# A two-branch spectral and gated-MLP kernel: transposes of nine row blocks moved to DMA, the row DFT one pass later, and the first unit's z differences on VectorE

## The chip, the cores and the metric

The kernel runs on one core of one Trainium2 chip. A core has five engines that run their own instruction queues and meet through semaphores: TensorE (PE; its weight loads are listed as PEld), VectorE (DVE), ScalarE (ACT), GpSimd (POOL) and SyncE (SP), which here only issues DMA transfers. ScalarE and GpSimd issue some transfers too. The metric is the device time of one execution in microseconds (us); lower is better. All times below come from runs of the kernel before, or from one profiled execution of it.

## The reference: what is computed

The input x is a matrix of 2048 rows by 576 columns, normalised row by row (xn). Two branches read xn. The first is a global filter: a two-dimensional real FFT, a product with a complex weight, and the inverse FFT. The second is a gated MLP with a product over the rows (w_sp). The result is x plus the first branch times the SiLU of the second:

```python
x = A_x
xn = _layernorm(x, axis=-1)
s = irfft2(rfft2(xn) * (w_r + 1j * w_i))               # branch A
z = gelu(xn @ w_in)                                    # 2048 x 4608
z1 = z[..., :Fh]; z2 = _layernorm(z[..., Fh:])         # Fh = 2304
g = w_sp @ z2 + b_sp[:, None]
g = silu((z1 * g) @ w_out)                             # branch B
return x + s * g
```

## The kernel before, in words

**Rows.** The 2048 rows are 16 blocks of 128 (MT = 16), called rows m here. A block is loaded into XC, normalised by VectorE into one of three buffers XN (m % 3), transposed, and kept as xnT for both branches. The steps of a row are:

- `ln1_stats` and `ln1_aggr` (lines 270 and 274): mean and variance on VectorE. The reciprocal root comes from GpSimd in two small instructions (`rstd_of`, lines 261 and 263), for row 0 from ScalarE and a VectorE reciprocal.
- `ln1_apply` (lines 293 and 296): two VectorE instructions write XN.
- `xpose` (lines 304 and 305): five TensorE transposes into PSUM, and a ScalarE copy into xnT.
- `p0_fold` (lines 311 and 312): sum and difference of the two halves of the row, on VectorE. Four buffers FS.
- `p0` (line 329), `p0_tail` (line 321), `p0_out` (lines 334 and 336): the DFT along the row as four full products and two row-tiled ones (64 rows each[...]), a ScalarE copy out of PSUM, and a store to DRAM that GpSimd issues.

**Column stages.** `p1` to `p5` do the DFT over the rows, the filter, and the inverse transforms, with DRAM in between. They are separated by stretches that only hold other work, so that the transfers can land.

**Chunks of branch B.** The products with w_in are 168 chunks: 96 of z2 (line 458, 384 columns wide, ordered by row) and 72 of z1 (line 554, which need all rows). The string `kinds` gives their order, and `fill(n, lead, tails, ahead)` issues the next n of them at a place in the program. Chunks go in groups of four: of the first two the full products, then one row-tiled pass for the remainders of all four, then the full products of the other two. What is given as `ahead` is issued before the row-tiled pass, and `tails` right behind it. After each chunk `z2_stats(lead)` may put statistics or normalisations of z2 on VectorE, as far as the sums kept by `spend` (the program's own estimate of the load of TensorE and VectorE) allow within `lead`.

**The row loop** (from line 781) does, for row m: fold of m, statistics of m + 3, normalisation of m + 2, and two chunks. An even row's `p0` comes between its two chunks, an odd row's ahead of them. Transposes run one row ahead. Four chunks are issued before the loop and 28 in it.

**The transition** (lines 856 to 873). After the column stages come the products with w_sp. They use sums and differences of quarters of w_sp ("slabs", brought in transposed by DMA; `slab_sums`, line 540, in three parts) and of z2 (`tsum`, lines 601, 603 and 605). `main(u)` (line 617) does unit u: seven groups of eight products into three PSUM tiles. Its fourth group adds to a tile that VectorE must have read first (the addition p1a, line 621), and uses the difference of line 603.

**Order.** The instructions of SyncE, TensorE and VectorE are in the order of the program text (`tc.manual_schedule`); those of ScalarE and GpSimd are ordered by the compiler's scheduler. Every engine runs its instructions in order.[...]

Of the kernel before, what the change touches and what calls it, by code (L numbers as in the profile page):

```python
# [90 lines left out]
def kernel(  # L91
# [138 lines left out]
    def load_win_main(t, fs, eng=nc.sync):  # L230
        for a in range(2):
            eng.dma_start(out=t[:, a:KS - 1:2, :], in_=wv[a, 0:2 * P, fs].rearrange("(b p) f -> p b f", p=P))
# [15 lines left out]
    for m0, m1 in ((0, 1), (1, 2), (2, 4)):  # L248
        nc.sync.dma_start(out=XC[0][:, m0:m1, :], in_=xv[:, m0:m1, :])
    for n in range(2):  # L250
        load_win_main(WIN2[:, :, n * ZC:(n + 1) * ZC], slice(Fh + n * ZC, Fh + (n + 1) * ZC), nc.scalar)
    for g in range(3):
        (load_win if g else load_win_tail)(WIN2[:, :, 2 * g * ZC:2 * (g + 1) * ZC], slice(Fh + 2 * g * ZC, Fh + 2 * (g + 1) * ZC))
        if g == 0:
            nc.sync.dma_start(out=CDSD, in_=cd_cdsd.ap().rearrange("p (a k l) -> p a k l", a=2, k=3))
        load_x(g + 1)
    nc.sync.dma_start(out=G1, in_=cd_g1.ap().rearrange("p (s k) -> p s k", s=N2))

    def rstd_of(mv, n, tag):
        ve = small.tile([P, n], F32, tag=tag + "v")  # L260
        nc.gpsimd.tensor_scalar(out=ve[:], in0=mv[:, :, 1], scalar1=1e-5, scalar2=one[:, 0:1], op0=ALU.add, op1=ALU.mult)
        rs = small.tile([P, n], F32, tag=tag + "r", bufs=5)
        nc.gpsimd.tensor_tensor(out=rs[:], in0=ve[:], in1=mhalf[:, 0:n], op=ALU.pow)
        return rs
# [7 lines left out]
    def ln1_aggr(m):  # L272
        mv = small.tile([P, 1, 2], F32, tag="mv1", bufs=5, name="mv1")
        nc.vector.bn_aggr(out=mv[:, 0, :], in_=st1[m][:])
        if m == 0:
            rs = small.tile([P, 1], F32, tag="l11r", bufs=5, name="rs1")
            nc.scalar.activation(out=rs[:], in_=mv[:, :, 1], func=ACT.Sqrt, bias=eps[:], scale=1.0)
        else:
            rs = rstd_of(mv, 1, "l11")
        ln1_of[m] = (mv[:, 0, 0:1], rs[:, 0:1])  # L280
# [4 lines left out]

    st1 = {}
# [13 lines left out]
    def xpose(m):  # L300
        xn = XN[m % 3]
        pt = psh.tile([P, KS, P], BF16, tag="h")
        for ks in range(KS):
            nc.tensor.transpose(pt[:, ks, :], xn[:, ks * P:(ks + 1) * P], ident[:])
        nc.scalar.activation(out=xnT[:, m, :, :], in_=pt[:], func=ACT.Identity)  # L305
# [287 lines left out]
    def tsum(u, which):  # L593
# [6 lines left out]
        if which == 0:  # L600
            nc.vector.tensor_tensor(out=t, in0=zblk(p, 1, 1), in1=zblk(p, 0, 1), op=ALU.subtract)
        elif which == 1:
            nc.vector.tensor_tensor(out=t, in0=t2, in1=zblk(p, 0, 0), op=ALU.subtract)
        else:
            nc.gpsimd.tensor_tensor(out=t, in0=zblk(p, 1, 0), in1=t2, op=ALU.subtract)  # L605
# [91 lines left out]
    kinds = "2" * 32 + "221" * 11 + "21" * 20 + "221" * 9 + "2111" * 4  # L697
# [42 lines left out]
    with tc.manual_schedule(engines={SP, PE, DVE}):  # L740
# [20 lines left out]
        nc.scalar.activation(out=THF[:, 0:1], in_=ln1_of[0][1], func=ACT.Gelu_apprx_tanh)  # L761
        xpose(0)
        ln1_stats(1, (1,))
        ln1_aggr(1)
        keep_warm(2)
        fill(1, 0)
        ln1(2)
        ln1_apply(1)
        p0_fold(0)
        ln1_apply(2)  # L770
        ln1(3)
        fill(1, 0, lambda: p0_pair(0), lambda: (xpose(1), p0(0, True), xpose(2)))
        p0_fold(1)
        ln1_apply(3)
        p0(1, False)
        p0_out(1)
        ln1(4)
        fill(1, 0)
        fill(1, 0)
        nc.sync.dma_start(out=MM, in_=cd_mm.ap().rearrange("p (a k) -> p a k", a=3))  # L780
        for m in range(2, MT):
            if m % 2 == 0:
                xpose(m + 1)
            spend(0.78, 2.35 if m + 3 < MT else 0.6)
            p0_fold(m)
            if m + 3 < MT:
                ln1(m + 3)
            if m + 2 < MT:
                ln1_apply(m + 2)
            if m % 2 == 0:  # L790
                fill(1, 0)
                p0(m, True)
                fill(1, 0, lambda: p0_pair(m))
            else:
# [3 lines left out]
                if m + 1 < MT:  # L798
                    xpose(m + 1)
                fill(1, 0)  # L800
            if m in (6, 9):
                load_win1(m // 9)
# [18 lines left out]
        for hh in range(0, N2, 2):  # L821
# [4 lines left out]
            if hh % 8 != 6:  # L826
                fill(1)
# [5 lines left out]
        for u in range(4 * NLC):  # L833
            p4(u)
            spend(0.45, 1.22 if u % 2 == 0 else 0)
            if u % 3 != 2:
                fill(1)
# [19 lines left out]
        for i in range(NT // P):  # L857
            fill(1, 2)
            slab_sums(i, 0, 1)
            spend(0, 0.75)  # L860
        later.append(partial(slab_sums, 2, 0, 2))
        fill(max(kinds.rindex("2") + 1 - place[0], 0), 2)
        nc.sync.dma_start(out=BB, in_=B_b_sp.rearrange("(a s) -> a s", a=1).to_broadcast((P, S)))
        fill(len(kinds) - place[0], 3)
        z1_store(None, None)
        tick[0] += 4
        z2_stats(99)
        assert not stats_q and not norm_q
        for w in (0, 2, 1):
            tsum(0, w)  # L870
# [51 lines left out]
```

## Time and profile before

| | us |
|---|---|
| median of 10 runs | 502.81 |
| lowest and highest | 502.15, 504.59 |
| profiled execution | 502.94 |
| its span on the core | 501.2 |
| TensorE busy | 488.6 |
| VectorE busy | 343.1 |
| GpSimd busy | 210.5 |
| ScalarE busy | 169.4 |

The span is the time from the first to the last instruction of the profiled execution; about 1.7 us of the execution lie around it. Busy times of TensorE are modelled: a matmul counts until its modelled end, so short waits don't show. The profile gives for each group of instructions the engine, the source line, what is written and read, and, in brackets, how long the engine stood idle before it and what released it. The granted clock of TensorE is at its full value throughout (0.998 on average). The transfers of the first 30 us keep the DMA engines busy; after that, up to the column stages, they are mostly idle.

### The profile page before, as it was taken

The page shows a single profiled execution, that of the slowest core. Times are in us where ns is not written, and L with a number is a line of the kernel's source. Part 1 is how long each engine was busy: PE and PEld are TensorE (multiplying, and loading weights), DVE is VectorE, ACT ScalarE, POOL GpSimd, SP SyncE. Part 2 cuts the span into 40 slices and gives each one's busy share as a digit, 9 for nine tenths or more (in the row PEclk, how much of TensorE's full clock was granted, in tenths as well). Part 3 has the DMA queues.
Part 4 walks back from the last instruction along what each step waited for, and adds up shares of the span by engine and source line. Part 5 has one row for each costly group of instructions (what it writes and reads, how often), then busy time and mean ns, then how long its engine had stood idle before and what let it go on. Part 6 is the DMA issues. An engine that isn't in the chain of part 4 may idle for free.

```text
span 501.2 us, 9370 instructions
## 1 busy us (share of the span) xinstructions
PE 488.6 (97%) x3454; PEld 308.7 (62%) x3454; DVE 343.1 (68%) x746; ACT 169.4 (34%) x355; POOL 210.5 (42%) x281
## 2 busy tenths in 40 slices
PE   6999999999999999799999999999999999999996
PEld 2555454555556544366666677666666678888885
DVE  5766588898655798966665547865656637877734
ACT  3887778686778556200000011000000011000001
POOL 2664323444242675554534501445354301666600
PEclk9999999999999999999999999999999999999999
DMA  7951688977362999771112499021111863111202
GB/s 233 335 174 61 221 290 238 333 226 231 125 232 91 241 229 269 212 232 60 35 33 64 115 159 233 25 63 33 40 57 33 173 135 94 50 48 45 79 27 70
DMA packets 86766, 70.67 MB, mean 141 GB/s; under 512 B 39776, under 2 KB 79328, under 8 KB 86464
## 3 DMA queue, kind: packets, MB, share of 16 engines
q1 hardware_dynamic: 80480, 55.54, 41.4%
q0 software_dynamic: 5008, 13.71, 8.3%
q10 hardware_dynamic: 1232, 0.82, 0.6%
q8 instruction: 27, 0.44, 0.3%
q14 instruction: 19, 0.16, 0.1%
HBM read 40.40 MB, written 21.26 MB: 123 GB/s over the span
## 4 chain that ended last, share of the span: by engine, by line
PE 88%; ACT 5%; DMA 3%; DVE 2%; issue 1%; SPq 0%; ACTq 0%; DVEq 0%
PE pm L617 42%; PE ph L554 13%; PE po L671 13%; PE ph L458 12%; ACT AR L334 2%; PE pb L386 2%; PE pa L329 2%; DMA AR<-in_A_x_dram 1%; ACT Z L477 1%; PE pa L428 1%; DMA Z1d<-AR 1%; PE pa L374 1%; ACT AR L305 1%; ACT Z L471 1%; DMA AR<-c_cdsd 1%
## 5 line engine op out<-in xcount | busy, mean ns | idle before, releaser
L617 PE MATMUL pm<-AR,Z 128*128 128x384 bf16 (+1 forms) x864 | 138.9, 309 | 0.0
L621 DVE TENSOR_TENSOR AR<-pm,AR 128x384 f32<-128x384 f32 (+3 forms) x162 | 82.4, 513 | 70.0 <-PE pm L617 66.8
L617 PE MATMUL pm<-AR 128*128 128x384 bf16 (+1 forms) x648 | 107.1, 309 | 2.9 <-DVE AR L621 2.3
L617 PEld LDWEIGHTS <-Z 128*128 128x128 bf16 x864 | 84.5, 98 | 40.6
L458 PE MATMUL ph<-AR 128*128 128x384 bf16 (+1 forms) x480 | 90.1, 327 | 1.8 <-ACT AR L305 0.9
L554 PE MATMUL ph<-AR 128*128 128x512 bf16 (+1 forms) x360 | 85.9, 380 | 0.0
L617 PEld LDWEIGHTS <-AR 128*128 128x128 bf16 x648 | 63.3, 98 | 33.9 <-issue 2.8
L631 ACT ACTIVATE AR<-pm 128x384 f32<-128x384 f32 (+1 forms) x27 | 12.3, 455 | 188.5 <-PE pm L617 188.5
L671 PE MATMUL po<-AR 128*128 128x288 bf16 x540 | 66.6, 287 | 0.0
L671 PEld LDWEIGHTS <-AR 128*128 128x128 bf16 x594 | 56.9, 98 | 14.0
L605 POOL TENSOR_TENSOR AR<-Z,AR 128x1024 bf16<-128x1024 bf16 x27 | 57.9, 2143 | 14.3 <-PE pm L617 13.4
L458 PEld LDWEIGHTS <-AR 128*128 128x128 bf16 (+1 forms) x480 | 40.0, 97 | 37.1 <-issue 15.6
L574 POOL DMA_DIRECT2D Z1d<-AR x55 | 32.0, 582 | 58.5 <-ACT AR L563 54.2
L632 POOL TENSOR_TENSOR AR<-AR 128x384 f32<-128x384 f32 (+1 forms) x27 | 22.9, 849 | 75.6 <-ACT AR L631 75.3
L554 PEld LDWEIGHTS <-AR 128*128 128x128 bf16 (+1 forms) x360 | 30.2, 97 | 28.1 <-issue 5.5
L563 ACT ACTIVATE AR<-ph 128x512 bf16<-128x512 f32 x72 | 42.1, 593 | 15.6 <-PE ph L554 15.4
L477 ACT ACTIVATE Z<-ph 128x384 bf16<-128x384 f32 x66 | 32.0, 502 | 24.6 <-PE ph L458 24.3
L674 ACT ACTIVATE TH<-po 128x576 f32<-128x576 f32 x15 | 9.8, 650 | 77.8 <-PE po L671 77.8
L635 POOL TENSOR_TENSOR AR<-AR 128x384 f32<-128x384 f32 (+1 forms) x27 | 30.4, 1126 | 12.7 <-DVE AR L621 12.6
L485 DVE BATCH_NORM_STATS2 st<-Z 128x6 f32<-128x384 bf16 x66 | 32.5, 545 | 1.5 <-ACT Z L477 1.5
L628 DVE TENSOR_TENSOR AR<-AR 128x384 bf16<-128x384 bf16 (+1 forms) x108 | 31.8, 336 | 0.9
L680 DVE SCALAR_TENSOR_TENSOR AR<-TH,po 128x576 bf16<-128x576 f32 x15 | 11.3, 755 | 30.0 <-ACT TH L674 29.9
(82 smaller groups left out, 476.8 us busy)
## 6 DMA issues: line engine op xcount, KB each, us to landing
Z1d<-AR POOLq DMA_DIRECT2D x55, 128.0 KB, 3.8
AR<-Z1d SPq DMA_DIRECT2D x36, 192.0 KB, 3.0
AR<-in_A_x_dram SPq DMA_DIRECT2D x18, 144.0 KB, 2.8
AR<-in_B_w_out_dram SPq DMA_DIRECT2D x1, 2592.0 KB, 9.9
Ad<-AR POOLq DMA_DIRECT2D x16, 144.5 KB, 3.0
AR<-Ad SPq DMA_DIRECT2D x4, 578.0 KB, 5.8
AR<-in_A_w_r_dram SPq DMA_DIRECT2D x16, 144.5 KB, 3.6
AR<-in_A_w_i_dram SPq DMA_DIRECT2D x16, 144.5 KB, 3.7
```

The costliest lines, as they stand in the source:

```text
L458: nc.tensor.matmul(self.ph[:], lhsT=xnT[rows, self.m, ks, :], rhs=WIN2[rows, ks, n * ZC:(n + 1) * ZC], start=start, stop=stop)
L477: nc.scalar.activation(out=zc, in_=ph[:], func=ACT.Gelu_apprx_tanh)
L485: nc.vector.bn_stats(out=z2s[m][:, n, :], in_=zc)
L554: nc.tensor.matmul(self.ph[:].rearrange("p (a t) -> p a t", a=4), lhsT=wb[rows, ks, (fi % WG) * P:(fi % WG + 1) * P], rhs=xnT[rows, 4 * tq ...
L563: nc.scalar.activation(out=zs, in_=ph[:], func=ACT.Gelu_apprx_tanh)
L574: (nc.sync if place[0] > len(kinds) - 16 else nc.gpsimd).dma_start(out=d, in_=s_)
L605: nc.gpsimd.tensor_tensor(out=t, in0=zblk(p, 1, 0), in1=t2, op=ALU.subtract)
L617: nc.tensor.matmul(dst, lhsT=z[:, s, :], rhs=SLB[SA[name]][:, s, 0:nt], start=(s == 0 and not more), stop=(s == HM - 1), skip_group_check= ...
L621: nc.vector.tensor_tensor(out=out, in0=x, in1=y, op=ALU.add)
L628: nc.vector.tensor_tensor(out=o, in0=o, in1=zb[:, f, h, 0:nt], op=ALU.mult)
L635: nc.gpsimd.tensor_tensor(out=ux, in0=p1a, in1=B[0], op=ALU.add)
L671: nc.tensor.matmul(pv[:, hh, :], lhsT=U[:, fi, h, i * P:(i + 1) * P], rhs=WOUT[:, fi, c0 + hh * H2:c0 + hh * H2 + w // nh], start=(fi == 0 ...
```

## The change

Four things are changed.

1. **Start.** The loads are re-ordered. The first weights of z2 come in halves between the first rows; ScalarE issues one of them where it issued four, and SyncE the other three. Row 3 comes behind the tails of the weights. The z1 weights of the first two groups follow the last rows directly; before, the constants G1 followed, then MM, and the z1 weights came at rows 6 and 9. G1 is now loaded in halves at rows 9 and 11, and MM after the loop. Rows 0 and 1 both take their root from ScalarE, and rows 2 and 3 take the addition of epsilon on VectorE. The first transpose is copied by VectorE.
2. **Row loop.** It begins with row 0, behind four chunks, and holds 32 chunks. Row m now folds m, normalises m + 4 and takes the statistics of m + 5. Transposes run three rows ahead. From row 7 (`DT`) on they are DMA transposes from XN to xnT, issued by SyncE, with no TensorE or ScalarE work. An even row's `p0` is given as `ahead`, so it comes behind both chunks' full products. `kinds` begins with 36 z2 chunks.
3. **Column stages.** Two chunks of the filter stage are issued later, and the chunks among the inverse products over the rows (`p4`) have a lead of 0.6.
4. **Transition.** The last z2 statistics and the first difference of unit 0 come before the last four chunks, the other two differences right behind these, and all three run on VectorE for unit 0.

```diff
@@ -227,8 +227,8 @@
     HT = H2 - 2 * P
     wv = B_w_in.rearrange("(a d) f -> a d f", a=2)
 
-    def load_win_main(t, fs, eng=nc.sync):
-        for a in range(2):
+    def load_win_main(t, fs, eng=nc.sync, halves=(0, 1)):
+        for a in halves:
             eng.dma_start(out=t[:, a:KS - 1:2, :], in_=wv[a, 0:2 * P, fs].rearrange("(b p) f -> p b f", p=P))
 
     def load_win_tail(t, fs):
@@ -245,20 +245,30 @@
         load_win(wb, fs)
 
     nc.scalar.dma_start(out=ident[:], in_=cd_id.ap())
-    for m0, m1 in ((0, 1), (1, 2), (2, 4)):
-        nc.sync.dma_start(out=XC[0][:, m0:m1, :], in_=xv[:, m0:m1, :])
-    for n in range(2):
-        load_win_main(WIN2[:, :, n * ZC:(n + 1) * ZC], slice(Fh + n * ZC, Fh + (n + 1) * ZC), nc.scalar)
+    wh = [(WIN2[:, :, n * ZC:(n + 1) * ZC], slice(Fh + n * ZC, Fh + (n + 1) * ZC)) for n in range(2)]
+
+    def load_row(m):
+        nc.sync.dma_start(out=XC[0][:, m, :], in_=xv[:, m, :])
+
+    load_row(0)
+    load_win_main(*wh[0], nc.scalar, (0,))
+    nc.scalar.activation(out=THF[:, 1:2], in_=eps[:], func=ACT.Sqrt)
+    load_win_main(*wh[0], nc.sync, (1,))
+    load_row(1)
+    load_win_main(*wh[1], nc.sync)
+    load_row(2)
     for g in range(3):
         (load_win if g else load_win_tail)(WIN2[:, :, 2 * g * ZC:2 * (g + 1) * ZC], slice(Fh + 2 * g * ZC, Fh + 2 * (g + 1) * ZC))
         if g == 0:
+            load_row(3)
             nc.sync.dma_start(out=CDSD, in_=cd_cdsd.ap().rearrange("p (a k l) -> p a k l", a=2, k=3))
         load_x(g + 1)
-    nc.sync.dma_start(out=G1, in_=cd_g1.ap().rearrange("p (s k) -> p s k", s=N2))
-
-    def rstd_of(mv, n, tag):
+    for g in range(2):
+        load_win1(g)
+
+    def rstd_of(mv, n, tag, eng=nc.gpsimd):
         ve = small.tile([P, n], F32, tag=tag + "v")
-        nc.gpsimd.tensor_scalar(out=ve[:], in0=mv[:, :, 1], scalar1=1e-5, scalar2=one[:, 0:1], op0=ALU.add, op1=ALU.mult)
+        eng.tensor_scalar(out=ve[:], in0=mv[:, :, 1], scalar1=1e-5, scalar2=one[:, 0:1], op0=ALU.add, op1=ALU.mult)
         rs = small.tile([P, n], F32, tag=tag + "r", bufs=5)
         nc.gpsimd.tensor_tensor(out=rs[:], in0=ve[:], in1=mhalf[:, 0:n], op=ALU.pow)
         return rs
@@ -272,17 +282,18 @@
     def ln1_aggr(m):
         mv = small.tile([P, 1, 2], F32, tag="mv1", bufs=5, name="mv1")
         nc.vector.bn_aggr(out=mv[:, 0, :], in_=st1[m][:])
-        if m == 0:
+        if m < 2:
             rs = small.tile([P, 1], F32, tag="l11r", bufs=5, name="rs1")
             nc.scalar.activation(out=rs[:], in_=mv[:, :, 1], func=ACT.Sqrt, bias=eps[:], scale=1.0)
         else:
-            rs = rstd_of(mv, 1, "l11")
+            rs = rstd_of(mv, 1, "l11", nc.vector if m < 4 else nc.gpsimd)
         ln1_of[m] = (mv[:, 0, 0:1], rs[:, 0:1])
 
     def ln1(m):
         ln1_stats(m)
         ln1_aggr(m)
 
+    DT = 7
     st1 = {}
     ln1_of = {}
 
@@ -297,12 +308,18 @@
                                 in0=xr[:, None, :, 2 * P:H2].to_broadcast((P, 2, 2, HT)), scalar1=mean, scalar2=rs,
                                 op0=ALU.subtract, op1=ALU.mult)
 
-    def xpose(m):
+    def xpose_dma(m):
+        nc.sync.dma_start_transpose(out=xnT[:, m, :, :], in_=XN[m % 3].rearrange("p (k i) -> p k i", k=KS))
+
+    def xpose(m, eng=nc.scalar):
         xn = XN[m % 3]
         pt = psh.tile([P, KS, P], BF16, tag="h")
         for ks in range(KS):
             nc.tensor.transpose(pt[:, ks, :], xn[:, ks * P:(ks + 1) * P], ident[:])
-        nc.scalar.activation(out=xnT[:, m, :, :], in_=pt[:], func=ACT.Identity)
+        if eng is nc.scalar:
+            nc.scalar.activation(out=xnT[:, m, :, :], in_=pt[:], func=ACT.Identity)
+        else:
+            eng.tensor_copy(out=xnT[:, m, :, :], in_=pt[:])
 
     Adw = Ad[:].rearrange("(c m p) l -> m p c l", c=2, p=P)
 
@@ -602,7 +619,7 @@
         elif which == 1:
             nc.vector.tensor_tensor(out=t, in0=t2, in1=zblk(p, 0, 0), op=ALU.subtract)
         else:
-            nc.gpsimd.tensor_tensor(out=t, in0=zblk(p, 1, 0), in1=t2, op=ALU.subtract)
+            (nc.gpsimd if u else nc.vector).tensor_tensor(out=t, in0=zblk(p, 1, 0), in1=t2, op=ALU.subtract)
 
     def main(u):
         it, p = units[u]
@@ -694,7 +711,7 @@
     zq = iter(range(MT * NZC))
     yq = iter(range(FT * 4))
     tick = [0]
-    kinds = "2" * 32 + "221" * 11 + "21" * 20 + "221" * 9 + "2111" * 4
+    kinds = "2" * 36 + "221" * 10 + "21" * 20 + "221" * 8 + "2111" * 4
     kinds += "2" * (MT * NZC - kinds.count("2")) + "1" * (FT * 4 - kinds.count("1"))
     held = []
     place = [0]
@@ -758,48 +775,49 @@
         ln1_stats(1, (0,))
         nc.vector.reciprocal(out=ln1_of[0][1], in_=ln1_of[0][1])
         ln1_apply(0)
-        nc.scalar.activation(out=THF[:, 0:1], in_=ln1_of[0][1], func=ACT.Gelu_apprx_tanh)
-        xpose(0)
         ln1_stats(1, (1,))
         ln1_aggr(1)
+        nc.scalar.activation(out=THF[:, 0:1], in_=ln1_of[1][1], func=ACT.Gelu_apprx_tanh)
+        xpose(0, nc.vector)
+        nc.vector.reciprocal(out=ln1_of[1][1], in_=ln1_of[1][1])
+        ln1_apply(1)
         keep_warm(2)
         fill(1, 0)
+        xpose(1)
         ln1(2)
-        ln1_apply(1)
-        p0_fold(0)
+        fill(1, 0)
+        ln1(3)
         ln1_apply(2)
-        ln1(3)
-        fill(1, 0, lambda: p0_pair(0), lambda: (xpose(1), p0(0, True), xpose(2)))
-        p0_fold(1)
-        ln1_apply(3)
-        p0(1, False)
-        p0_out(1)
         ln1(4)
         fill(1, 0)
+        ln1_apply(3)
+        xpose(2)
         fill(1, 0)
-        nc.sync.dma_start(out=MM, in_=cd_mm.ap().rearrange("p (a k) -> p a k", a=3))
-        for m in range(2, MT):
-            if m % 2 == 0:
-                xpose(m + 1)
-            spend(0.78, 2.35 if m + 3 < MT else 0.6)
+        for m in range(MT):
+            if m % 2 == 0 and m + 3 < DT:
+                xpose(m + 3)
+            spend(0.9 if m + 3 < DT else 0.6, 0.5 + 0.6 * (m + 4 < MT) + 1.0 * (m + 5 < MT))
             p0_fold(m)
-            if m + 3 < MT:
-                ln1(m + 3)
-            if m + 2 < MT:
-                ln1_apply(m + 2)
+            if m + 4 < MT:
+                ln1_apply(m + 4)
+                if m + 4 >= DT:
+                    xpose_dma(m + 4)
+            if m + 5 < MT:
+                ln1(m + 5)
             if m % 2 == 0:
                 fill(1, 0)
-                p0(m, True)
-                fill(1, 0, lambda: p0_pair(m))
+                fill(1, 0, lambda: p0_pair(m), lambda: p0(m, True))
             else:
                 p0(m, False)
                 p0_out(m)
                 fill(1, 0)
-                if m + 1 < MT:
-                    xpose(m + 1)
+                if m + 3 < DT:
+                    xpose(m + 3)
                 fill(1, 0)
-            if m in (6, 9):
-                load_win1(m // 9)
+            if m in (9, 11):
+                hf = slice((m - 9) * N2 // 4, (m - 7) * N2 // 4)
+                nc.sync.dma_start(out=G1[:, hf, :], in_=cd_g1.ap().rearrange("p (s k) -> p s k", s=N2)[:, hf, :])
+        nc.sync.dma_start(out=MM, in_=cd_mm.ap().rearrange("p (a k) -> p a k", a=3))
         for ch in range(4):
             p1_read(ch)
         load_w(0)
@@ -823,7 +841,7 @@
             if hh + 2 < N2:
                 p2(hh + 2)
                 spend(0.25, 1.5)
-            if hh % 8 != 6:
+            if hh % 8 != 6 and hh < 26:
                 fill(1)
             p3(hh)
             spend(0.5)
@@ -834,7 +852,7 @@
             p4(u)
             spend(0.45, 1.22 if u % 2 == 0 else 0)
             if u % 3 != 2:
-                fill(1)
+                fill(1, 0.6)
         js = [4 * g + r + 2 * h for g in range(MT // 4) for r in range(2) for h in range(2)]
         slabs = [(a, i) for i in range(NT // P) for a in (0, 2, 1, 3)]
         for n in range(0, MT, 2):
@@ -854,20 +872,20 @@
                 slab_sums((n - 6) // 4, 0, 0)
                 spend(0, 1.5)
         load_z1(0)
-        for i in range(NT // P):
-            fill(1, 2)
-            slab_sums(i, 0, 1)
-            spend(0, 0.75)
-        later.append(partial(slab_sums, 2, 0, 2))
-        fill(max(kinds.rindex("2") + 1 - place[0], 0), 2)
-        nc.sync.dma_start(out=BB, in_=B_b_sp.rearrange("(a s) -> a s", a=1).to_broadcast((P, S)))
-        fill(len(kinds) - place[0], 3)
-        z1_store(None, None)
         tick[0] += 4
         z2_stats(99)
+        tsum(0, 0)
+        later.append(partial(slab_sums, 2, 0, 2))
+        assert place[0] > kinds.rindex("2")
+        nc.sync.dma_start(out=BB, in_=B_b_sp.rearrange("(a s) -> a s", a=1).to_broadcast((P, S)))
+        for i in range(NT // P):
+            fill(1)
+            slab_sums(i, 0, 1)
+        fill(len(kinds) - place[0])
+        z1_store(None, None)
+        for w in (1, 2):
+            tsum(0, w)
         assert not stats_q and not norm_q
-        for w in (0, 2, 1):
-            tsum(0, w)
         for i in range(2):
             slab_sums(i, 0, 2)
         nc.sync.dma_start(out=WOUT, in_=B_w_out.rearrange("(f p) d -> p f d", p=P))
```

## The prediction

> **What bounds the kernel now.** I read the busy row of TensorE over the span first, then busy times by stage, then the chain of waits inside each stage where TensorE is not full.
>
> ```profile
> PE   6999999999999999799999999999999999999996
> 0.00:15.00 15.00, 10.62 (x59) 4.88 (x60) 8.61 (x32) 7.30 (x12) 3.48 (x14) 1.00 0.81 247
> 15.00:51.00 36.00, 35.42 (x292) 20.97 (x291) 25.50 (x91) 28.54 (x56) 22.31 (x39) 1.00 0.58 176
> 200.00:215.00 15.00, 12.21 (x70) 6.17 (x68) 14.35 (x21) 3.42 (x7) 8.84 (x8) 1.00 0.77 235
> ```
>
> The windows' columns are PE, PEld, DVE, ACT and POOL busy, granted clock, DMA share, GB/s. The kernel is TensorE work from end to end except in two places: the first 15 us (4.4 us idle) and 200 to 215 us (2.8 us idle). The change touches both, and the stage between 15 and 51 us, the row DFT, which looks full. There the chain shows a short wait that the busy time hides, because matmul ends are modelled:
>
> ```profile
> 20.26 0.61 ACT AR L305
> 20.86 0.02 issue
> 20.89 0.30 DVE AR L311
> 21.19 0.05 issue
> 21.24 0.67 PE pa L329 x4
> ```
>
> This is one row's path: ScalarE copies the transposed row (L305), VectorE folds it (L311), TensorE multiplies (L329). The fours of L329 for even rows stand at 21.24, 26.44, 31.65, 36.85, 42.05 and 47.26: 5.20 us for a pair of rows. TensorE's last instruction before 21.24 starts its four matmuls at 20.33, and four of these take 0.65 from start to start elsewhere (18.47 to 19.12), so it waits 0.26 us. Of the other 4.94, two groups of five transposes take 0.28 each (24.32 to 24.60). Without them a pair costs 4.38.
>
> Next, VectorE at the start of the stage, where it once has the order that the changed loop will have throughout:
>
> ```profile
> 11.95 0.21 DVE L274 BATCH_NORM_AGGREGATE mv<-st 128x2 f32<-128x12 f32 x1
> 12.08 0.24 DVE L311 TENSOR_TENSOR AR<-AR 128x256 bf16<-128x256 bf16 x1
> 13.32 0.41 DVE L293 TENSOR_SCALAR AR<-AR,mv,rs 128x512 bf16<-128x512 bf16 x1 [0.80 <-POOL rs L263]
> 13.87 0.81 DVE L270 BATCH_NORM_STATS2 st<-AR 128x6 f32<-128x288 bf16 x2
> 14.72 0.21 DVE L274 BATCH_NORM_AGGREGATE mv<-st 128x2 f32<-128x12 f32 x1
> 15.03 0.38 POOL L261 TENSOR_SCALAR ve<-mv,one 128x1 f32<-128x1 f32 x1 [1.75 <-DVE mv L274]
> 15.50 0.55 POOL L263 TENSOR_TENSOR rs<-ve,mhalf 128x1 f32<-128x1 f32 x1
> ```
>
> Statistics, fold, then the normalisation of that same row, which waits for GpSimd's reciprocal root: 1.37 us from the aggregate at 11.95 to the normalisation at 13.32. GpSimd's result for the next row, at 16.05, is 1.33 us behind its aggregate. In the rest of the stage another row's work lies between the two and nothing waits.
>
> Last, the 2.8 us at 206 to 211:
>
> ```profile
> 206.25 2.57 POOL L605 TENSOR_TENSOR AR<-Z,AR 128x1024 bf16<-128x1024 bf16 x1 [2.53 <-PE pm L617]
> 206.75 2.61 DVE L540 TENSOR_TENSOR AR<-AR 128x1024 bf16<-128x1024 bf16 x1
> 210.60 0.54 DVE L621 TENSOR_TENSOR AR<-pm,AR 128x384 f32<-128x384 f32 x1
> 211.20 1.46 PE L617 MATMUL pm<-AR 128*128 128x384 bf16 x8 [2.26 <-DVE AR L621]
> ```
>
> TensorE waits for the addition L621, which stands behind two block sums (L540) on VectorE. One of these takes 2.61 us beside a GpSimd difference; alone they take 0.63.
>
> [...]
>
> **The change, part by part.**
>
> 1. Start. The loads are re-ordered: row 0, half of the first weights, row 1, the rest. ScalarE issues one weight load in place of four, so its table load (3.35, 1.28 us) comes about 1.7 us earlier; row 0's root still waits for its aggregate, which ends at 4.21, and gains 0.4 us at most. But row 1's statistics stand on VectorE ahead of row 0's reciprocal, and row 1 now has 392 KB of weights ahead of it. At about 250 GB/s (the first 15 us show 247) it lands near 5.3 instead of 3.7. So row 0 is normalised near 6.0 (5.17 before), and the first product is near 7.9 (7.10). VectorE copies transpose 0 from PSUM; nearest row, ScalarE's 0.68. Later this start loses less: the weight waits at 8.14 and 9.13 and the constants' wait at 11.09 (0.9 and 0.6 us) go, since both come earlier. What decides is rows 4 to 7 (590 KB): the bytes ahead of them are the same as before, where they landed at 12.7; their issue comes about a microsecond sooner, so I take 12.1. Row 4's statistics then start at 12.1, its normalisation at 14.4, row 5's statistics at 15.0. Before, row 5's started at 15.20. For VectorE the start is a wash, with 1 us either way.
>
> 2. Row loop. Each iteration is now: fold of row m, normalisation of m+4, statistics of m+5. On VectorE's queue the statistics of a row are followed by one fold and then by the normalisation of that row. That is the order seen at 11.95. One row costs 0.85 (statistics to aggregate) + 1.37 + 0.55 (normalisation to the next statistics, 13.32 to 13.87) = 2.77 us, 5.54 per pair, against 5.20 now. From row 5 to row 15: 15.0 + 10 x 2.77 = 42.7. GpSimd is in order too, and issuing one DFT store costs it 0.75 (two in 1.49). The order of instructions puts a store between the two steps of rows 6 and 14 (0.75 each) and stores of rows 4 to 6 ahead of row 11, the last of which needs row 6's product; I take 1.0. That makes 45.2 for row 15's statistics, 42.12 before.
>
> Behind it: the fold of row 11 ends 1.4 later, 46.6; then its products and two chunks (0.5 + 1.3) and two pairs at 4.38, which makes 57.2. Before, at that amount of work: products of row 15 at 49.19, with the two chunks 51.0, and the four chunks that the new stage holds more (4 x 0.65 + 0.43) make 54.0. So the stage loses 3.2 us, although 45 transposes (9 x 0.28 = 2.5 us of TensorE) and nine ScalarE copies are gone: they are taken out of a stage that then waits for VectorE. Moving an even row's products behind the second chunk removes the 0.26 us wait, already counted in 4.38.
>
> 3. The nine DMA transposes. SyncE reaches the first behind the twelve loads of the first z1 weights, which now follow x directly. SyncE stalls with eight outstanding (the last z1 weights went out at 27.51, when the 1 MB load issued at 17.72 landed), so I take 26.8 for its turn. Each then costs SyncE between 0.8 us (1.30 for the w_sp ones, scaled from 1,024 to 640 columns)[...]. I take 0.9 and 3 us to land (w_sp: 3.2 to 8.0, median 4.4). Row 7 lands near 30 and its buffer is wanted near 31.9: hidden. The rest follow at VectorE's pace. Of the moved loads, G1 and MM are wanted at 61 us or later: hidden.
>
> 4. Transition. From 202.29 VectorE does two block sums, a difference, three sums, two differences, two sums: 7 x 0.63 + 3 x 0.71 = 6.5, 208.8, then the addition, 209.35. GpSimd's bias addition (1.08 us at 209.05 before) will now run beside some of these: up to 0.7 more (the second L540 ran to 1.39 beside it). I take 209.7 for the waiting products, a gain of 1.5. Next late is still the same addition: two sums stay ahead of it.
>
> 5. Fill chunks taken from the column stages are spent later, same number; the smaller lead of the fills among the inverse column products may save some of the 0.5 us that TensorE waits at 150 to 160. I take 0.4 for this.
>
> Sum: +3.2 - 1.5 - 0.4 = +1.3 us on the profiled execution's 502.94 (span 501.2 plus 1.7 around it), which is 0.13 above the median of the runs: **504.1**.
>
> **The rivals.**
>
> - TensorE-bound row loop (faster). If GpSimd's root returned within a fold (0.4 us), VectorE would need 1.8 to 1.9 a row and TensorE decides: from 14.2, 4.66 + 4.94 + 6 x 4.38 gives 50.1, a gain of 3.9, with the rest 5.8: 497.1. For it: 45 transposes less and the chain's own path cut. Against: both 1.37 and 1.33.
> - GpSimd's stores don't hit (no change). Without their 2.5 us the stage loses 0.7, and the total is 501.7, at the edge of no change. For it: row 11's wait rests on one product's time.
> - Slow transposes (much slower). The last must land before row 15's products at 55.6, so 26.8 + 9s + 3 decides from s = 2.9 us per issue; at 3.5 the stage ends 6.2 later still: 510.3. For it: [...]single issues of 2.65 in the trace. Against: a median of 1.30.
>
> **How the numbers follow.** Chances: forecast 0.50, stores hidden 0.20, TensorE-bound 0.18, slow transposes 0.12. The forecast's own range is 502.8 to 506.3 (start 1 us either way, GpSimd 1 us, transition 0.5). The range 499.5 to 508.5 leaves out about half of the first and last rivals. Slower by over 0.2% (1 us, about what can be told from no change): nine tenths of the forecast and slow transposes, 0.56; within: 0.20; faster: TensorE-bound and a third of the stores' case, 0.24.
>
> **What would show it.** In the new profile: normalisations in the row loop idle "<-POOL rs", rows 2.8 us apart, TensorE's products of odd rows waiting for the fold; no wait on the transposes; the products after the first unit's third waiting about 0.8 us instead of 2.26. If rows follow at 2.2 us, steps 2 and its stores are wrong. If the first chain item behind a fold is a DMA, step 3 is.

## The result and the profile after

The changed kernel takes 512.83 us (median of 9 runs, 511.90 to 513.71); the kernel before, in the runs beside it, 502.48. The ratio is 1.0196, with a 95% interval of 1.0179 to 1.0212: some 10 us slower, where 504.1 was forecast and 508.5 was the upper end of the range. The profiled execution has a span of 510.6 us, 9.4 more than before. Each experiment below ran beside the kernel before, whose median lay between 501.35 and 502.48 us, so kernels are compared by their ratios.

TensorE's row of the page shows two new places. The second to fourth of its 40 slices (13 to 51 us, the row loop) have 8, 7 and 7 tenths where the kernel before has 9. In the sixth (64 to 77 us) the engine first stands still and then has a slow clock:

```profile
PE   6877969999999999999999999999999999999997
PEclk9999979999999999999999999999999999999999
```

Five stretches of the changed kernel, with PE, PEld, DVE, ACT and POOL busy, granted clock, DMA share and GB/s:

```profile
64.00:68.00 4.00, 3.61 (x22) 1.60 (x20) 0.00 (x0) 3.97 (x12) 2.11 (x4) 1.00 0.44 142
68.00:72.00 4.00, 0.22 (x2) 0.13 (x2) 0.00 (x0) 0.46 (x2) 0.54 (x1) 0.76 0.78 245
72.00:76.00 4.00, 4.00 (x14) 1.84 (x13) 1.30 (x3) 1.25 (x2) 0.54 (x1) 0.50 1.01 413
76.00:80.00 4.00, 4.00 (x24) 2.02 (x23) 2.43 (x5) 2.73 (x5) 0.82 (x2) 0.89 0.61 157
208.00:222.00 14.00, 13.37 (x80) 6.45 (x79) 12.38 (x24) 5.66 (x11) 6.46 (x10) 1.00 0.74 226
```

From 68 to 72 us TensorE does next to nothing (it waits 4.17 us, up to 71.78); from 72 to 76 it counts as full, but with 14 matmuls where 24 follow in the next 4 us, at a clock of 0.50. The last line is the transition, which has become better: 0.6 us idle, where the kernel before had 2.8.

The two waits by name (in total, times, longest) are TensorE's for the folds of the row loop and its wait ahead of `p1`:

```profile
PE pa L346 <- DVE AR L328: 7.0, 6, 1.9
PE pa L367 <- DMA AR<-Ad: 4.2, 1, 4.2
```

The chain of waits of the changed kernel tells where the 4 us come from (start, length, what):

```profile
53.90 8.30 DVE st L502 x18
...
62.22 0.33 DVE mv L518
...
62.65 0.26 POOL ve L271
...
62.99 0.48 POOL rs L273
...
63.52 0.45 POOL Ad L353
...
64.27 0.56 POOL Ad L353
...
64.99 2.82 DMA Z1d<-AR
67.81 3.93 DMA AR<-Ad
...
71.78 0.64 PE pa L367 x2
72.42 1.71 PE ph L571 x4
```

Read it backwards. The first product of `p1` (L367) waits for a reading of Ad (67.81); the readings wait for the last stores of Ad (L353, the chain names the landing by the store of Z1d that is next in the queue); and these two stores, of rows 14 and 15, are issued at 63.52 and 64.27, although row 15's products end near 57. They stand in GpSimd's queue behind the reciprocal root (L271, L273) of the second norm's row 0. That root needs VectorE's aggregate (L518), which needs 18 statistics that VectorE could only begin behind its last fold. In the kernel before, the same two stores were issued at 50.77, ahead of that root at 57.12:

```profile
50.77 1.55 POOL L336 DMA_DIRECT2D Ad<-AR  x2 [3.73 <-ACT AR L334]
...
57.12 0.26 POOL L261 TENSOR_SCALAR ve<-mv,one 128x1 f32<-128x1 f32 x1 [1.71 <-DVE mv L501]
```

No line of the change touches either; GpSimd's order is the compiler's.

In the row loop the forecast's picture is there. VectorE's timeline, with the idle time before an instruction in brackets:

```profile
36.41 0.41 DVE L304 TENSOR_SCALAR AR<-AR,mv,rs 128x512 bf16<-128x512 bf16 x1 [1.98 <-POOL rs L273]
...
39.19 0.41 DVE L304 TENSOR_SCALAR AR<-AR,mv,rs 128x512 bf16<-128x512 bf16 x1 [0.81 <-POOL rs L273]
...
45.52 0.41 DVE L304 TENSOR_SCALAR AR<-AR,mv,rs 128x512 bf16<-128x512 bf16 x1 [1.60 <-POOL rs L273]
...
53.41 0.29 DVE L328 TENSOR_TENSOR AR<-AR 128x256 bf16<-128x256 bf16 x1 [2.83 <-DMA AR<-AR]
```

A row's normalisation waits 0.8 us for GpSimd, more where a store stands between, and the last fold waits 2.83 us for a DMA transpose.

To compare whole kernels I counted TensorE's lost time: the time from the first matmul to a stage's first product, less what the matmuls in between need at 2.4 columns a nanosecond, half of it for row-tiled ones. Both are estimates from the trace of the changed kernel: four matmuls of 512 columns take 0.86 us from start to start (209.61 to 210.47 us), which is 2.38 columns a nanosecond, and four row-tiled ones of 384 columns take 0.34 us (55.40 to 55.74), where sixteen full ones take 2.60 (52.21 to 54.81). The twelve warm-up products at the start count as lost. Lost time in us, stage by stage, in one profiled execution each:

| kernel | row stage | to p1 | p1 to p2 | p2 to p4 | p4 to p5 | p5 to w_sp | behind |
|---|---|---|---|---|---|---|---|
| before | 12.8 | 0.8 | 2.4 | 4.0 | 2.1 | 2.4 | 8.7 |
| after | 19.2 | 5.2 | 4.6 | 4.2 | 2.9 | 2.4 | 6.8 |
| stores on SyncE | 19.3 | 0.8 | 2.1 | 4.2 | 2.9 | 2.3 | 6.5 |
| statistics first | 12.2 | 7.4 | 5.0 | 4.3 | 2.9 | 2.3 | 6.8 |
| both mends | 11.7 | 0.8 | 2.1 | 4.2 | 2.8 | 2.4 | 9.6 |
| no DMA transposes | 16.3 | 0.8 | 2.1 | 4.3 | 2.9 | 2.3 | 6.5 |
| before, normalisation first | 16.4 | 0.8 | 2.4 | 4.0 | 2.1 | 2.4 | 8.1 |
| transition alone | 11.9 | 0.8 | 2.4 | 4.0 | 2.1 | 2.4 | 6.5 |

The 45 transposes that went to DMA save 2.4 us of work (45 x 53 ns, 128 columns at that pitch; in the trace of the kernel before five take 0.28 us, 24.32 to 24.60, or 56 ns each). So after against before: +6.4 - 2.4 = +4.0 in the row stage, +4.3 in the wait ahead of p1, +2.2 in the slow clock, +0.2 from p2 to p4, +0.8 in p4, -1.9 in the transition: +9.6, beside 9.4 in the spans. The last row and the first are the same program for 200 us, and their row stages differ by 0.9. The version with both mends and its three variants at the end share the text of the row stage too, and lose 11.7, 11.7, 12.0 and 13.1 us there. So a difference of under some 1.4 us between the row stages of two executions tells nothing.

### The profile page after: what moved, and what is told of

It reads as the page before. It is cut to its first block, busy times and chain, and to the rows that moved or that the text cites. A ratio compares the mean times of both kernels' runs of the same rounds, so it can differ in the third digit from the quotient of the medians.

```text
span 510.6 us, 9300 instructions
## 1 busy us (share of the span) xinstructions
PE 488.6 (96%) x3409; PEld 307.2 (60%) x3409; DVE 342.0 (67%) x751; ACT 164.2 (32%) x347; POOL 206.1 (40%) x276
## 4 chain that ended last, share of the span: by engine, by line
PE 81%; DVE 8%; DMA 4%; POOL 2%; issue 2%; ACT 1%; SPq 1%; DVEq 0%; POOLq 0%; ACTq 0%
PE pm L634 42%; PE po L688 13%; PE ph L571 12%; PE ph L475 8%; DVE st L280 2%; DVE st L502 2%; PE pb L403 2%; POOL rs L273 1%; PE pa L367 1%; PE pa L445 1%; PE pa L391 1%; DVE AR L304 1%; DMA AR<-AR 1%; DMA AR<-Ad 1%; POOL ve L271 1%
## 5 line engine op out<-in xcount | busy, mean ns | idle before, releaser
L475 PE MATMUL ph<-AR 128*128 128x384 bf16 (+1 forms) x480 | 88.9, 330 | 0.3 <-DVE AR L322 0.3
L622 POOL TENSOR_TENSOR AR<-Z,AR 128x1024 bf16<-128x1024 bf16 x26 | 55.3, 2127 | 12.1 <-PE pm L634 11.3
```

The lines of the kernel that those rows point to most:

```text
L475: nc.tensor.matmul(self.ph[:], lhsT=xnT[rows, self.m, ks, :], rhs=WIN2[rows, ks, n * ZC:(n + 1) * ZC], start=start, stop=stop)
L622: (nc.gpsimd if u else nc.vector).tensor_tensor(out=t, in0=zblk(p, 1, 0), in1=t2, op=ALU.subtract)
```

## The experiments

**The two late stores issued by SyncE.**

```diff
-        nc.gpsimd.dma_start(out=Adw[m], in_=sg[:, :, 0:L])
+        (nc.sync if m >= MT - 2 else nc.gpsimd).dma_start(out=Adw[m], in_=sg[:, :, 0:L])
```

> The changed kernel (512.8 us) with the p0_out stores of the last two rows, 14 and 15, issued by SyncE instead of GpSimd; nothing else differs. Theory A (queue order: in the changed kernel these two stores stand in GpSimd's queue behind the reciprocal root of the second norm's row 0, which waits for VectorE's 18 statistics, so they issue at 63.5 us where the products of row 15 ended at about 57): the stores issue by about 58, the four readings p1_read start near 59 to 60 and land near 63, TensorE's 4.2 us wait ahead of p1 (L367) and the half clock of 72 to 76 us go, and the time falls by 5 to 7 us, to 506 to 508. Theory B (p1 is late because the row loop itself is late, and the stores only mirror it): under 1 us is gained, and another wait stands ahead of p1.

506.89 us, ratio 1.0101 (1.0081 to 1.0121). SyncE issues both at 57.46, GpSimd's root comes at 63.19, about as late as in the changed kernel (62.65):

```profile
57.46 1.04 SPq L353 DMA_DIRECT2D Ad<-AR  x2
...
61.56 2.07 SPq L359 DMA_DIRECT2D AR<-Ad  x4
```

In the profiled execution, the fastest of the six, the wait ahead of p1 and the slow clock are gone, and nothing else in the table has moved. Two of the other runs have a mean clock of 0.992 and 0.993, as low as the changed kernel's 0.993, so the clock falls somewhere in them too; where was not profiled. Theory A holds: the queue order cost 0.0095 of the ratio, about 5 us, and 6.7 us in the spans of the two profiled executions.

**Dummy work in the wait.**

```diff
         fill(11)
+        keep_warm(20)
```

> The changed kernel (512.8 us) with keep_warm(20), 20 matmuls of 128x512 on data that nobody reads, behind fill(11) and so in the 4.2 us in which TensorE waits for the readings of p1: some 4.3 us of work that adds nothing, in a gap that stays as long. Theory A (the half clock of 72 to 76 us follows from TensorE's standing still, and costs about 2.2 us on top of the wait): the wait stays, the granted clock stays near 1.00 through 80 us, and 1.5 to 2.3 us are saved: 510.5 to 511.3. Theory B (the clock falls for another reason, such as the burst of DMA that follows the stores): the clock still falls there, and the time is 512.5 to 513.5.

510.89 us, ratio 1.0173 (1.0143 to 1.0202). The wait is filled, and the clock stays:

```profile
68.00:72.00 4.00, 4.00 (x19) 1.71 (x18) 0.00 (x0) 0.34 (x1) 0.54 (x1) 1.00 0.81 242
72.00:76.00 4.00, 3.92 (x26) 2.12 (x26) 2.01 (x4) 2.45 (x5) 0.70 (x2) 1.00 1.02 415
```

The burst of DMA is that of the changed kernel (415 GB/s, 413 there) and the clock is 1.00, so theory B falls. From p1 to p2 2.5 us are lost instead of 4.6. The mean clock of its five runs is 0.996 to 1.000; that of the changed kernel's nine is 0.993 or less in eight. The gain in the time is 1.9 us by the medians and 1.2 by the ratios, and the intervals overlap; the clock is what decides. From what length of gap on the clock falls was not shown: it fell in the gap of 4.17 us, and with both mends, below, it also falls behind one of 2.24 us.

**Statistics between a row's aggregate and its normalisation.**

```diff
             p0_fold(m)
+            if m + 5 < MT:
+                ln1(m + 5)
             if m + 4 < MT:
                 ln1_apply(m + 4)
                 if m + 4 >= DT:
                     xpose_dma(m + 4)
-            if m + 5 < MT:
-                ln1(m + 5)
```

> The changed kernel with VectorE's row turn in the order fold(m), ln1(m+5), ln1_apply(m+4) instead of fold(m), ln1_apply(m+4), ln1(m+5): the statistics of the next row stand between a row's aggregate and the normalisation that needs GpSimd's root of it. The stores of rows 14 and 15 stay behind the root in GpSimd's queue. Theory A (the round trip to GpSimd sets the row loop's 2.77 us period): the waits of VectorE for the root (11.9 us in 12) all but vanish, the period falls to about 2.2 us or to what TensorE allows, the last products of row 15 end 3 to 4 us sooner, and if the wait ahead of p1 is tied to VectorE's own chain (fold(15), 18 statistics, root, stores) it moves forward by the same: 508 to 510. Theory B (TensorE or ScalarE bounds the row loop, VectorE's waits lie beside it): under 1 us.

507.32 us, ratio 1.0098 (1.0075 to 1.0121), a little better than expected. VectorE's row now is:

```profile
24.86 0.81 DVE L280 BATCH_NORM_STATS2 st<-AR 128x6 f32<-128x288 bf16 x2
25.70 0.21 DVE L284 BATCH_NORM_AGGREGATE mv<-st 128x2 f32<-128x12 f32 x1
25.83 0.37 DVE L304 TENSOR_SCALAR AR<-AR,mv,rs 128x512 bf16<-128x512 bf16 x1
```

No idle time before L304, and 1.89 us from one row's normalisation to the next (23.94, 25.83). The row stage loses 12.2 us instead of 19.2. But GpSimd's queue has the stores behind the root still, and the wait ahead of p1 has grown, since TensorE arrives sooner:

```profile
PE pa L367 <- DMA AR<-Ad: 6.4, 1, 6.4
```

Two defects in series: mending the first lengthens the second by 2 us.

**Both mends**, the two edits above together.

> The two edits together: stores of rows 14 and 15 on SyncE, and the statistics of row m+5 ahead of the normalisation of row m+4 on VectorE. Theory (row loop and hand-over are the two losses, the transition the gain): the loop ends 3 to 4 us sooner and p1 follows it without a wait, so 502 to 504 falls out of 512.8 minus 6 minus 3.5, about equal to the kernel before or 1 us over. Rival (p1 is then held by VectorE's or by DMA's next wait): 505 to 507.

499.36 us, ratio 0.9949 (0.9932 to 0.9966): faster than the kernel before and than expected, and 0.0054 of the ratio (2.7 us) better than the two gains added, since the wait that grew is gone too. What a row loop bounded by TensorE is worth is seen here: 11.7 us lost and 2.4 us less work than before, 3.5 us (2.1 in the variant with 13.1 us lost). In the profiled execution, the slowest of the nine (501.15 us), part of it is given back at the transition (9.6 us lost behind it, against 6.5):

```profile
205.07 1.48 PE L634 MATMUL pm<-AR 128*128 128x384 bf16 x8 [2.24 <-DVE AR L557]
206.38 2.73 PE L634 MATMUL pm<-AR,Z 128*128 128x384 bf16 x8
```

The chunks of first products have run out before VectorE has the block sums of w_sp (L557), three of which stand behind the first difference. Behind the wait the first eight products take 1.48 us and the next eight 2.73: the clock has fallen again.

```profile
204.00:208.00 4.00, 2.93 (x14) 1.55 (x15) 4.00 (x8) 0.00 (x0) 1.60 (x1) 0.80 0.65 233
208.00:212.00 4.00, 4.00 (x21) 2.14 (x20) 3.11 (x4) 0.00 (x0) 2.60 (x3) 0.77 0.56 154
```

That is 1.7 us of full clock missing, and takes the mean clock of this execution to 0.997. The other eight have 0.998 to 1.000, so a fall of this length happened in this one alone, and the median doesn't hold it.

**The transition alone**, put into the kernel before: the change's lines from `load_z1(0)` to the last `tsum`, and the difference on VectorE for unit 0.

> The kernel before with the change's transition part alone: z differences of unit 0 on VectorE, first of them ahead of the last w_sp block sums, and the fills behind z2_stats(99) reordered as in the change. Theory (the transition is the one part that gains, about 2 us of TensorE idle in the trace): 500.3 to 501.0 us beside 502.5, so 1.5 to 2.2 us less. Rival (the gain needs the changed loop's other order of fills, or comes with the earlier bias load only): within 0.5 us of before.

500.11 us, ratio 0.9962 (0.9948 to 0.9976), a gain of 1.9 us. Which of the transition's edits brings it was not tried one by one. TensorE's wait of 2.26 us is gone, and what is left is the shorter one that was always there:

```profile
205.26 1.47 PE L617 MATMUL pm<-AR 128*128 128x384 bf16 x8 [0.53 <-ACT AR L631]
```

**No DMA transposes.**

```diff
-    DT = 7
+    DT = MT
```

> The changed kernel with DT = MT: the nine transposes of rows 7 to 15 go back to TensorE and ScalarE, SyncE issues none. Theory A (they are hidden, and VectorE's round trips to GpSimd set the row loop): TensorE gets about 9 x 0.5 us more to do in a loop where it has waits of 7 us for VectorE, so the time stays within 1.5 us of 512.8. Theory B (the slow transposes hold back the last rows: VectorE's waits of 0.3 and 2.8 us ahead of fold(14) and fold(15) set the end of the loop and, through the 18 statistics behind them, GpSimd's root and the stores): 2 to 3 us are saved, 510 to 511.

504.90 us, ratio 1.0053 (1.0035 to 1.0071): some 7 us saved by the ratios, which neither theory had. GpSimd's timeline tells why:

```profile
57.13 1.45 POOL L353 DMA_DIRECT2D Ad<-AR  x2 [2.93 <-ACT AR L351]
59.01 0.26 POOL L271 TENSOR_SCALAR ve<-mv,one 128x1 f32<-128x1 f32 x1 [0.43 <-DVE mv L518]
```

The last two stores now stand ahead of the root. Up to that root's aggregate VectorE has the same instructions in the same order in both kernels (later some z2 statistics move, since `DT` also enters the program's estimate of the load). So it is the change's move of transposes to DMA that makes the compiler turn the two around, and this is most of what the move costs. Why the compiler reckons so was not tried. The row stage itself is the same within what one execution tells: 2.9 us less lost, 2.4 us more work.

**Both at once**: stores on SyncE and `DT = MT`.

> The changed kernel with both the stores of rows 14 and 15 on SyncE and DT = MT (no transposes on the DMA queues). Stores on SyncE alone gave 506.9 (ratio 1.0101), DT = MT alone 504.9 (1.0053); in the latter the stores stand ahead of the second norm's root in GpSimd's queue, though nothing in their code was changed. Theory A (both take away the same wait ahead of p1, DT = MT by way of the order in GpSimd's queue, and the transposes cost about 2 us of their own at the end of the row loop): the two don't add up, and the time is that of DT = MT alone, 504.3 to 505.5. Theory B (they are two losses): 512.8 minus 6 minus 8, about 499.

504.43 us, ratio 1.0068 (1.0056 to 1.0081), as theory A has it: the two remove the same wait. Against the stores on SyncE alone (1.0101) that is 0.0033, or 1.7 us, for the transposes by themselves; the intervals touch at 1.0081, so it lies between nothing and 3 us, and the slow clock in two runs of the former may be part of it. They save TensorE work that this loop has no use for, and hold up the last fold by 2.83 us.

**Both mends without DMA transposes** (`DT = MT` there).

> The version with both mends (499.4 us: stores of rows 14 and 15 on SyncE, statistics ahead of the normalisation) with DT = MT, that is with no transposes on the DMA queues. There TensorE has no waits from 15 to 60 us, so what it gets back is paid. Theory A (the DMA transposes are worth their TensorE time in a loop that TensorE bounds): 9 times 5 transposes of some 55 to 60 ns and their share of loads, 2.5 to 4 us slower: 502 to 503.5. Theory B (their landing, up to 4.5 us of wait on VectorE, costs as much as they save): within 1 us of 499.4.

500.80 us, ratio 0.9971 (0.9958 to 0.9985). The ratio is 1.1 us worse than with them, between the two theories and within the intervals. In the traces p1's first product comes 2.7 us later, as the work says, and behind the w_sp products' start 6.7 us are lost instead of 9.6: in these two executions what the transposes save is given back there. The fall of the clock is part of the 9.6, so the median run with them may keep more.

**The normalisation first, in the kernel before.**

```diff
-            if m + 3 < MT:
-                ln1(m + 3)
             if m + 2 < MT:
                 ln1_apply(m + 2)
+            if m + 3 < MT:
+                ln1(m + 3)
```

> The kernel before with VectorE's row turn turned the other way: ln1_apply(m+2) ahead of ln1(m+3), so that a row is normalised right behind its own aggregate, as in the changed kernel. Theory (the round trip to GpSimd's root, about 0.8 us a row and more where a store stands in GpSimd's queue, is what made the changed loop longer): VectorE gets 13 such waits, some 0.8 us each and 10 to 12 us in all, of which its 1.3 us of idle time per pair of rows takes up to 8: 2 to 5 us slower than before, 504 to 507. Rival (the order on VectorE matters only together with the DMA transposes and the earlier rows of the change): within 1 us of 502.

505.84 us, ratio 1.0090 (1.0076 to 1.0104): 4.5 us slower by the order of two calls. VectorE's waits (in total, times, longest):

```profile
DVE AR L293 <- POOL rs L263: 13.6, 14, 1.5
```

Its row stage loses 3.6 us more than before; the changed kernel's, 4.0 net. So this order alone is enough to explain the changed row loop.

**Three tries to better the version with both mends.** First, four chunks are kept for later (`fill(11)` ahead of p1 and `fill(12)` ahead of p2):

```diff
-        fill(11)
+        fill(9)
...
-        fill(12)
+        fill(10)
```

> The version with both mends with fill(9) instead of fill(11) ahead of p1 and fill(10) instead of fill(12) ahead of p2: four of the 168 chunks of first products are kept for the end of the column stage. In that version TensorE waits 2.2 us at 205 us for the first-unit differences on VectorE, because the products that covered them have run out, and the granted clock is 0.94 behind it; p1's readings land near 57.9 and p2's near 82.9, about 2 us ahead of their use. Theory (the gain of a shorter loop is given back at the end for want of cover): 2 to 3.5 us saved, 496 to 497.5. Rival (p1 and p2 then wait as long for their readings): within 0.7 us of 499.4.

500.91 us, ratio 0.9981 (0.9968 to 0.9995): no gain, where 496 to 497.5 was expected. The wait at the transition went from 2.2 us to none, but between p2 and p4 6.9 us are lost instead of 4.2, in waits for ScalarE's GELU copies out of PSUM.

Second, in the loop of p5, where each of two `fill(1)` becomes:

```diff
-            fill(1)
+            fill(n < MT - 2)
```

> The version with both mends (499.4 us) with one chunk of first products taken from between the last two p5 calls and put behind them, so that the last column work ends about 0.9 us sooner and TensorE has that much more to do until VectorE has the first-unit differences. Theory (the 2.2 us wait at 205 us is the time from the last p5, by way of the last Yd store, to the differences): the wait falls by 0.9 to 1.3 us and the time to 498.2 to 498.8. Rival (the Yd stores behind a busy DMA set it, not the last p5): within 0.5 us of 499.4.

499.20 us, ratio 0.9962 (0.9948 to 0.9976). The wait fell to two of 0.8 us; the time can't be told from 499.4.

Third, in p4:

```diff
-                fill(1, 0.6)
+                fill(1)
```

> The version with both mends (499.4 us, ratio 0.9949) with the fills among p4 at the lead of the kernel before (fill(1) instead of fill(1, 0.6)). In every kernel that holds the change, TensorE waits 0.9 us once in p4 (L419), for a ScalarE copy or a load, where the kernel before waits 0.3 us in all. Theory A (the smaller lead moves VectorE's or ScalarE's work against p4): that wait goes, 0.5 to 0.9 us saved. Theory B (it comes from the chunks that now stand elsewhere in the order, whose ScalarE work meets p4's copies): the 0.9 us wait stays, and the time is within 0.5 us of 499.4.

499.75 us, ratio 0.9969 (0.9954 to 0.9984), and the wait of 0.9 us in p4 stays: theory B. With the lead ruled out, the chunks' new order is the likeliest cause left; it wasn't tried by itself.

So the version with both mends and the one with the transition alone beat both kernels, the kernel before by 2.6 and 1.9 us by their ratios; which of them is the better is not settled by these runs.

## Why the prediction was wrong

**The bound, and step 2 (row loop): right.** Forecast: VectorE's round trip to GpSimd sets 2.77 us a row, with stores of GpSimd in the way at rows 6, 11 and 14, a loss of 3.2 us. Measured: 2.76 us from row to row (39.19 to 41.95), 0.81 us of it a wait, more at row 6 (1.63), row 11 (1.98) and row 14 (1.60), in all 12 waits and 11.9 us, and a loss of 4.0. Undoing it took 7.0 us out of the row stage, 3.0 of these beyond the loop of before; bringing it about in the kernel before cost 4.5 us of time. The rival of a loop bound by TensorE (497.1) was wrong for the change as it stands, but is what the mended order gives. The rival in which the stores don't hit is wrong.

**Step 1 (start): within its 1 us.** Row 5's statistics start at 15.56, 15.0 in the forecast. VectorE waits 1.5 us for ScalarE ahead of row 1's reciprocal, which the step did not have. Row 15's statistics start at 46.06, 45.2 in the forecast, most of it this offset.

**Step 3 (DMA transposes, "hidden"): this is the step that failed, and not by the price; with it, the sum put the hand-over from the row stage to p1 at nothing, without a reason.** The runs showed 4.3 us of waiting there and 2.2 us of slow clock behind it, both gone without the DMA transposes. Issue took 1.23 us (0.9 assumed) and landing 2.9 (3 assumed), well short of the 2.9 us an issue from which the slow-transposes rival decides. The longest issue in the trace of the kernel before, of w_sp's 32, took 2.65 us; a price above that was my estimate, and no run showed it. Two things were left out. Small: the last two land late, 0.34 and 2.83 us of VectorE's time ahead of fold(14) and fold(15). Large: with them the compiler orders GpSimd's queue so that the last two stores come behind the root of the second norm. The prediction read GpSimd's order for the stores of rows 6, 11 and 14, but not for the last two. I priced the stores that stand between the steps of a row's root, since I was looking for what delays the root, and did not ask the reverse: what does the root delay, and when can it run at all? Its operand comes behind VectorE's last fold and 8.3 us of statistics. The answer is stores at 63.5 for products that end at 57. The sum ended the row stage at its last product.

**Nothing in the sum for the clock.** The wait of 4.17 us cost 2.1 us more than its length (4.6 us lost from p1 to p2, 2.5 where dummy work filled it). In the version with the statistics first the wait was 6.4 us, the clock was 0.50 from 64 to 72 us, and 5.0 were lost from p1 to p2. So where a forecast for this kernel holds a wait of TensorE of 4.2 to 6.4 us, the slow clock behind it belongs to its price.

**Step 4 (transition): right**, with a gain of 1.5 forecast and 1.9 measured, alone and in the change. The forecast left 0.8 us of the wait for the addition standing; the trace has a third of that, as in this part of TensorE's timeline of the changed kernel:

```profile
217.68 1.47 PE L634 MATMUL pm<-AR 128*128 128x384 bf16 x8 [0.53 <-ACT AR L648]
218.99 1.46 PE L634 MATMUL pm<-AR,Z 128*128 128x384 bf16 x8
220.55 1.46 PE L634 MATMUL pm<-AR 128*128 128x384 bf16 x8
```

The group at 220.55 is the one that waited 2.26 us. It starts 1.56 us behind the group ahead of it, where that one followed its own by 1.31: some 0.25 us of wait. The 0.53 was there before.

**Step 5 (fills): wrong sign.** A gain of 0.4 was guessed; p4 loses 0.8 more than before in every kernel with the change's order of chunks, for example here, in TensorE's timeline of the changed kernel. The profile names a load as what ended this wait; in most of the other kernels it names a ScalarE copy (L426), so the cause stays open:

```profile
164.47 0.61 PE L419 MATMUL pa<-AR 128*128 128x128 bf16 x8 [0.94 <-DMA AR<-in_B_w_in_dram]
```

The corrected sum is +4.0 + 4.3 + 2.2 + 1.0 - 1.9 = +9.6; without the hand-over and the clock it would have been +3.1.

## What to carry to other kernels

When a change moves work among queues, read each in-order queue at the end of the stage for what is urgent and stands behind something that isn't: here a store that the next stage waits for, behind a root that is needed later and can only run late. An edit elsewhere can turn such a pair around where a scheduler sets the order, so a short issue on a queue whose order you write yourself is the safer place (here SyncE, 1.04 us for the two stores). The round trip to GpSimd cost nothing where enough other work stood between its two ends (in the mended order some 1.9 us covered the 1.37 us here), and what was left uncovered was paid at every turn (0.8 us behind a fold alone).

## What the hardware showed that I had not expected

The granted clock fell inside a TensorE wait of 4.17 us and stayed low for some 5 us behind its end (1.00 from 69 to 70 us, 0.56 from 70.0 to 70.5, 0.50 up to 76.5, 0.62 from 76.5 to 77.0, 1.00 from there; the wait ended at 71.78): 0.76, 0.50 and 0.89 in three stretches of 4 us lose as much as 6.8 us at 0.50. In the version with both mends a wait of 2.24 us was enough in the profiled execution, and the clock fell only behind the wait (0.80 and 0.77 over 8 us lose as much as 3.4 us at 0.50), while the kernel before had a wait of 2.26 us with the clock at 1.00 through it: at this length both were seen. DMA transposes of 128x640 two-byte elements from SBUF to SBUF took SyncE 1.23 us to issue (median of nine) and landed in 2.9, up to 4.3.
